# A new table of issue order and engine choice for block-causal attention with a feed-forward layer

## The chip, the cores and the metric

The kernel runs on one core of a Trainium2 chip. The metric is the device time of one execution in microseconds. The engines are named as in the profile: PE is the matmul engine (PEld its weight loads), DVE the vector engine, ACT the scalar engine, POOL the GpSimd engine; SP is a queue that only issues DMAs. ACT issues DMAs too.

## What is computed

Eight batches of eight heads, 576 positions, head size 64, float32. Attention is causal by blocks of 64, the result is laid out as 4608 tokens of 512 features, and a feed-forward layer of width 2048 follows, `(h * clip(h+3,0,6) / 6) @ w_out`.

```python
scores = scale * np.matmul(q, k.transpose(0, 1, 3, 2))
scores = np.where(block_i >= block_j, scores, -1e9)
attn = np.exp(scores - scores.max(-1, keepdims=True))
attn = attn / (attn.sum(-1, keepdims=True) + 1e-09)
x = np.matmul(attn, v).transpose(0, 2, 1, 3).reshape(B * S, H * D)
h = x @ w_in
out = (h * np.clip(h + 3.0, 0.0, 6.0) / 6.0) @ w_out
```

## The kernel before

float32 values are split into a high and a low float16 part, and a product is three float16 matmuls (high*high, high*low, low*high). Each is issued as two matmuls of 64 columns of the array side by side, which the profile shows as 128*64.

The work is cut two ways. Attention goes by slots: one slot is a pair of heads of one batch, 32 in all. The feed-forward layer goes by 13 pieces of up to 384 tokens, each with 16 column blocks f of 128. The first batch (slots 0 to 3) and the first piece are computed in float32 matmuls while the weights still arrive. A slot, with the tile names that the profile uses:

- loads `qk`, `vnat` (in the first batch `qf`, `qr`, `vnat`); `qk_prep` (line 727) splits q and k into `qks` and a transposing DMA on SP makes `qkT`;
- `s_group` (976): score matmuls `s`, maxima `st` on DVE, exponentials `p` on ACT, a POOL memset on `p`, the split into `phl` (high part on ACT or DVE, low part on DVE), a transposing DMA on SP to `pT` (`t_dma`, 1066);
- `pv_group` (1090): matmuls `pv`, and the split of the result into the piece's `x`.

The first batch has instead `sf`, `pf`, transposes `pt` on PE, copies `pT`, row factors `rd`, `rb`, and matmuls `pr` and `pf`. Weights arrive in 32 loads (`w_load`, 526: `rawi`, `rawo` or a borrowed `x` buffer). Each is taken through `exi`/`exo` on ACT and `sgi`/`sgo` on DVE or POOL into `win`/`wout`; later `w_split` (614) makes the high part on DVE, ACT or POOL and the low part on DVE. A block of a piece is `ffn1` (1304): matmuls `h`, `r` on ACT, `r` on DVE, `g` high on ACT or DVE, `g` low on DVE; then `ffn2` (1352): matmuls `o` into three PSUM buffers, and after the 16th block `osb` and the store. Pieces 11 and 12 use a product scheme with fewer matmuls (`h_pair`, 1244: tiles `m`, `hf`, `hu`; its operands `wr`, `wq`, `ws`, `xr`, `xt` from `w_comb` and `x_comb`). Forty matmuls on zeros (`warm`, 1599) are strewn into the beginning.

None of this order reaches the chip directly. A recorder notes 6437 steps in the order of the program, each with the engines that may do it (`scaled`, 275, `load`, 299, `plus`, 1193). The table `ORDER` (78 to 209) is a packed list of all 6437 step numbers with an engine for each, and `schedule` (340) issues them so:

```python
for lo, hi in zip(raw[:half], raw[half:]):
    o = self.ops[lo + 256 * (hi % 32)]
    o.eng = self.NAMES[hi // 32]
```

Each engine works its steps in the order of the table. DMAs stand in it too, on SP or ACT, and are issued in that order; a DMA that waits holds up all that stands behind it on its queue. PSUM is small: scores and `pv` rotate through 3 buffers, `h` through 2, `o` has 3 of its own.

Of the kernel before, what the change touches and what calls it, by code (L numbers as in the profile page):

```python
# [17 lines left out]
P = 128  # L18
# [6 lines left out]
U = 2.211  # L25
# [20 lines left out]
GA = 5  # L46
# [24 lines left out]
QP = 0.573  # L71
# [12 lines left out]
    "1q%xn{e3JWuPFQFtL?YQwHlh{aAX$QM>Ci#HfMufnT`7_traU39HPu^W7Zp3Q1;&mv?P(O{2cukdo0<#&Z?Dby&)^pC&(gT=|<~i"
    "Yn+@@j8hLT&#suwGqEZE!ZR^78~b2cc`?n98th_3qr0YiZkph`d57HdI&jE0BXp1HU9+|8s)~xMYf8fA&6yv5zipM~>WKB@rJ*0$"
    "Ik}Ucyz@UdUTe6zxi&8{yeT61-|-N2E#11pS%mW!+G9Jm)W^lYKAf<1?>^4OOPBixeP%}uY)ec^4!hFXwVivS=as^f{F9l!#yiek"
    "i0*3Y&dusQoOi_U>9gxMZr*x+yYOhti@w9z1v#-t6<Md>oPYB2*htT*W8M96Q%BAW|NZ{sC-aw-bl=&cZ@q7~D5uR6djI?BrQ^>A"
    "76|`)@bJ-)jEL-?caP`H)gG18N!1e-R>8}k)4xg-!>g%kJSX@sR#|clr(}3toOHuLf~-1!>DOh-)#kMeZ`#>YmrGJ^eZRlrnEudR"
    "CnE>iLp_lP&bJ-u_l`3Txwv*7+3HZ^?)J#z@f~8F<*xYjgjI>F*Ccsnj3x7{QoQ<eUk{vEnQrl>y0)g?Dq!3AV6kq;$-SrcZC|yc"
    "B=DW%uv5<b1v`UwmA-8`y?f6@*+}`{ipk0g4UHQ&?bq4-zO`+^!uA6P^O~Jy<eG&PPRhzFo;f@9L+$4;^%pOHYv3Nf%GLbyLFwZt"  # L90
    "mt;V;wy_ocWGpslN13H%&lCS_XkvQt(Vn(eiKCKKBPkj~n$9%y^$zp*%9zid$I5Fyu{b^<arT@`No&`w=WpOFSeQI_na}0A{55`y"
    "_G<6TTypS$i>ur6mGuQH_PZb2c>Y}B(tx6d{F34;Wu-xZ9>Ja=St+kl%R{p}w`_{6OiK@sh>DKc9a~Y=xN7U>rjV{}J6CVt(Y^CV"
    "&#pIDU%%bccCF=l@4FlAc$JY4s>2_L`W`=ddi&J8`NAT<r*6K#d#hD6u49(^v(ulRpLucrtgM{8!a~J+pI_3n=6ty``}?=AxCcL!"
# [1543 lines left out]
```

## Time and profile before

| | |
|---|---|
| Time, median of 3 runs | 986.66 us (985.13 to 988.3) |
| Span of the profiled execution | 983.9 us |
| PE busy | 967.0 us (98%) |
| DVE busy | 861.1 us (88%) |
| ACT busy | 667.7 us (68%) |
| POOL busy | 107.7 us (11%) |

The span runs from the first to the last instruction, so the profiled execution is 2.8 us under the median. Nearly all instructions have one line, L362, the helper that issues every step, so that groups are told apart by their tiles. PE counts as busy from a matmul's start to its modelled end; a busy PE can still be waiting, and the distance from one matmul to the next tells more.

### The profile page before, as it was taken

What the parts mean: (1) busy time and instruction counts of PE and PEld (TensorE: products, weight loads), DVE (VectorE), ACT (ScalarE), POOL (GpSimd) and SP (SyncE); (2) the same over time, 40 slices, a digit from 0 to 9 for tenths busy, and PEclk for the clock granted to TensorE, in tenths of its full rate; (3) what the DMA queues carried; (4) which work ended last, traced back from release to release, by engine and by line L of the source; (5) the groups of instructions that cost most, each with busy time, mean ns of one, the idle gap of its engine ahead of it and who ended that gap; (6) DMA issues with size and microseconds to landing.
All of it is one profiled execution on the core that took longest, in us unless ns stands there. A gap on an engine that the chain in (4) does not pass through costs nothing.

```text
span 983.9 us, 31140 instructions
## 1 busy us (share of the span) xinstructions
PE 967.0 (98%) x12625; PEld 702.0 (71%) x12625; DVE 861.1 (88%) x2330; ACT 667.7 (68%) x1610; POOL 107.7 (11%) x280
## 2 busy tenths in 40 slices
PE   8999999999999999999999999999999999999998
PEld 5676666677878876677677776777667766878774
DVE  5899999999998999999999888977888779986863
ACT  4788877877777677878776777677776564444423
POOL 1354210000100000100000010001100113000000
PEclk9999999999999999999999999999999999999999
DMA  8975479989779598898998697958566632000000
GB/s 234 296 224 152 85 149 158 176 154 201 135 124 218 99 184 161 162 165 155 160 162 151 124 176 124 154 113 157 98 143 118 108 71 47 2 33 3 35 2 34
DMA packets 407184, 129.04 MB, mean 131 GB/s; under 512 B 393984, under 2 KB 396544, under 8 KB 407040
## 3 DMA queue, kind: packets, MB, share of 16 engines
q1 hardware_dynamic: 399824, 121.75, 64.9%
q10 hardware_dynamic: 7216, 5.29, 1.9%
q8 instruction: 99, 1.62, 0.7%
q14 instruction: 45, 0.37, 0.1%
HBM read 45.09 MB, written 9.44 MB: 55 GB/s over the span
## 4 chain that ended last, share of the span: by engine, by line
PE 41%; DVE 7%; ACT 2%; DMA 1%; issue 1%; ACTq 0%; POOL 0%; DVEq 0%; POOLq 0%
PE o L362 18%; PE h L362 12%; PE m L362 5%; PE s L362 2%; PE pv L362 2%; DVE st L362 2%; DVE phl L362 1%; DVE g L362 1%; DVE r L362 1%; DMA pT<-phl 1%; ACT p L362 1%; DVE xt L362 0%; DVE x L362 0%; DVE ws L362 0%; ACT phl L362 0%
## 5 line engine op out<-in xcount | busy, mean ns | idle before, releaser
L362 PE MATMUL o<-wout,g 128*64 128x512 f16 (+3 forms) x3336 | 426.5, 378 | 1.7 <-ACT osb L362 1.4
L362 PE MATMUL h<-x,win 128*64 128x384 f16 (+2 forms) x3952 | 376.0, 319 | 0.8 <-DVE r L362 0.7
L362 PEld LDWEIGHTS <-win 128*64 128x64 f16 (+1 forms) x4440 | 259.9, 110 | 73.4 <-issue 1.6
L362 PEld LDWEIGHTS <-g 128*64 128x64 f16 x3360 | 204.7, 110 | 102.6 <-issue 1.7
L362 ACT ACTIVATE p<-s,st,esc 128x384 f32<-128x384 f32 (+5 forms) x280 | 163.0, 586 | 57.0 <-DVE st L362 45.0
L362 DVE SCALAR_TENSOR_TENSOR phl<-p,st,phl 128x256 f16<-128x256 f32 (+4 forms) x252 | 141.4, 581 | 7.2 <-ACT phl L362 6.5
L362 ACT ACTIVATE r<-h,eg,sh 128x384 f32<-128x384 f32 (+1 forms) x192 | 112.2, 598 | 43.7 <-PE h L362 40.2
L362 ACT ACTIVATE phl<-p,st 128x256 f16<-128x256 f32 (+4 forms) x190 | 103.3, 577 | 40.6 <-DVE st L362 21.0
L362 DVE TENSOR_REDUCE st<-s 128x1 f32<-128x384 f32 (+6 forms) x280 | 120.3, 447 | 7.5 <-PE s L362 7.0
L362 ACT ACTIVATE g<-r 128x384 f16<-128x384 f32 (+1 forms) x160 | 79.8, 504 | 56.3 <-DVE r L362 42.8
L362 DVE SCALAR_TENSOR_TENSOR g<-r,g 128x384 f16<-128x384 f32 (+1 forms) x192 | 103.2, 543 | 10.4 <-ACT g L362 9.8
L362 DVE SCALAR_TENSOR_TENSOR r<-r,eg,h 128x384 f32<-128x384 f32 (+1 forms) x160 | 93.6, 587 | 10.3 <-ACT r L362 9.5
L362 PE MATMUL s<-qkT 128*64 128x512 f16 (+7 forms) x1120 | 100.8, 287 | 0.6 <-DMA qkT<-qks 0.2
L362 PEld LDWEIGHTS <-vhl 128*64 128x64 f16 x1680 | 77.3, 110 | 19.4 <-issue 3.4
L362 PE MATMUL pv<-pT,vhl 128*64 128x192 f16 (+2 forms) x1680 | 85.2, 233 | 2.2 <-DVE x L362 1.1
L362 PEld LDWEIGHTS <-qkT 128*64 128x64 f16 x1120 | 59.0, 110 | 26.8 <-issue 3.1
L362 POOL MEMSET p<- 128x64 f32 x140 | 21.1, 160 | 480.0 <-DVE phl L362 368.5
L362 ACT ACTIVATION_READ_ACCUMULATOR p<-s,st,esc 128x1 f32 x280 | 55.2, 197 | 0.0
L362 ACT ACTIVATE r<-hf,eg,sh 128x192 f32<-128x192 f32 (+1 forms) x48 | 26.8, 593 | 40.1 <-DVE hf L362 32.9
L362 DVE SCALAR_TENSOR_TENSOR qks<-qk,rs_q,qks 128x576 f16<-128x576 f32 x56 | 46.0, 836 | 0.3
L362 PE MATMUL m<-x,ws 128*64 128x192 f16 x768 | 40.3, 246 | 0.1
L362 PEld LDWEIGHTS <-ws 128*64 128x64 f16 x768 | 35.3, 110 | 5.9 <-DVE hf L362 0.3
(196 smaller groups left out, 1056.6 us busy)
## 6 DMA issues: line engine op xcount, KB each, us to landing
out_dram<-osb SPq DMA_DIRECT2D x34, 256.0 KB, 2.8
qk<-in_q_dram SPq DMA_DIRECT2D x28, 288.0 KB, 4.2
vnat<-in_v_dram SPq DMA_DIRECT2D x60, 128.0 KB, 3.0
qk<-in_k_dram SPq DMA_DIRECT2D x26, 288.0 KB, 3.8
rawo<-in_moe_w_out_dram SPq DMA_DIRECT2D x11, 512.0 KB, 5.6
rawi<-in_moe_w_in_dram SPq DMA_DIRECT2D x6, 512.0 KB, 5.4
x<-in_moe_w_in_dram SPq DMA_DIRECT2D x6, 512.0 KB, 6.0
pT<-phl SPq DMA_TRANSPOSE x140, 3.9
```

The lines of the kernel that those rows point to most:

```text
L362: getattr(eng, method)(*args, **kw)
```

## The change

Only the table differs. The steps, their operands and buffers, and everything outside `ORDER` are the same.

```diff
 ORDER = (
-    "c-l=`1zc0_*QYxMj1m<XY;2767+}%eBW=1nRSdejRZK()lTuL-ySv3suv=2!^W4Gj{hw|3KF|5aInTY^yE{Kl%E-#g32DtypRJ)e"
...
```

Unpacked, both tables hold each of the 6437 steps once. Their order differs from the first entry on, and all five engines' sequences differ. 390 steps have another engine. The table below counts them by the matmul work that stands ahead of them in the old table (in us, a matmul counted as its columns at the dense distance in time that the rows below show).

| from, to | 0 to 50 | 50 to 200 | 200 to 700 | 700 to 922 |
|---|---|---|---|---|
| DVE to ACT | 8 | 28 (`phl` 14, `qks` 4, `g` 4, `x` 3, `pT` 2, `rb` 1) | 59 | 9 |
| DVE to POOL | 8 (`sgi` 4, `sgo` 4) | 8 (`qks` 4, `win` 2, `sgo`, `wout`) | 7 | 5 (`wr`) |
| ACT to DVE | 12 (`pT` 8) | 11 (`phl` 5, `g` 3) | 99 (`phl` 43, `g` 32, `x` 13) | 50 (`g` 25) |
| POOL to DVE | 2 | 2 | 1 | 2 |
| ACT to POOL | 7 (`rd`) | 17 (`wout` 6, `rd` 5, `win` 3, `qks` 3) | 9 | 0 |
| POOL to ACT | 10 | 5 | 0 | 0 |
| DMA, ACT to SP | 20 | 2 | 0 | 0 |
| DMA, SP to ACT | 9 | 0 | 0 | 0 |

The beginning of the two DMA queues (the digit is the slot, the letter the tensor where a tile holds both):

| | first entries |
|---|---|
| ACT before | vnat0, vnat0, qf0 q, qf0 k, vnat1, qf1 q, qf1 k, qr0 q, qr0 k, qr0 k, vnat2, rawi, then `p`, qf2 q, ... |
| ACT after | qf0 q, qr0 q, qf0 q, qf1 k, qf1 q, vnat1, qf1 q, qf2 k, qf2 k, then `p`, `p`, `p`, exi, ... |
| SP before | vnat0, qf0 q, qf0 k, vnat1, vnat1, qf1 q, qf1 k, qr0 q, vnat2, vnat2, qf2 q, qf2 k, rawi, ... |
| SP after | vnat0, qf0 k, qf0 k, vnat2, qr0 q, qf1 k, rawi, vnat3, vnat2, vnat2, qf2 q, qr0 k, qf2 q, qr0 k, vnat1, ... |

On PE 15 `warm` matmuls stand ahead of the first `qt` before, 31 after. At the end PE's last block group is `o` buffer 0 (512 columns wide, stored whole) before, and `o` buffer 2 (256 wide, its two halves done by ACT and DVE) after.

## Rows read from the trace of the kernel before

**Rows 1.** The page: busy time by engine; 40 slices of the span.
```profile
PE 967.0 (98%) x12625; PEld 702.0 (71%) x12625; DVE 861.1 (88%) x2330; ACT 667.7 (68%) x1610; POOL 107.7 (11%) x280
...
DVE  5899999999998999999999888977888779986863
...
PEclk9999999999999999999999999999999999999999
```
**Rows 2.** Busy time by stage: stretch, then PE, PEld, DVE, ACT, POOL, clock, DMA, GB/s.
```profile
0.00:70.00 70.00, 63.83 (x710) 44.72 (x711) 54.35 (x156) 47.09 (x131) 24.03 (x56) 1.00 0.84 254
70.00:233.00 163.00, 160.95 (x1872) 111.41 (x1872) 160.11 (x469) 131.92 (x328) 29.78 (x66) 1.00 0.79 152
233.00:980.00 747.00, 742.12 (x10049) 545.90 (x10045) 646.63 (x1708) 488.02 (x1151) 53.86 (x159) 1.00 0.64 115
```
**Rows 3.** Chain that ended last, three dense pieces: start, length, what, matmuls.
```profile
555.23 3.88 PE o L362 x36
...
571.20 0.97 PE h L362 x12
...
936.06 0.99 PE m L362 x24
```
**Rows 4.** Groups by shape: matmuls of the largest groups; busy, mean ns of one.
```profile
L362 PE MATMUL o<-wout,g 128*64 128x512 f16 x3156 | 396.6, 379 | 1.7 <-ACT osb L362 1.4 <-DVE g L362 0.3
L362 PE MATMUL h<-x,win 128*64 128x384 f16 x3456 | 330.2, 326 | 0.4 <-DVE r L362 0.2
```
**Rows 5.** Who DVE waited for, 70 to 233 us: total, times, longest.
```profile
DVE st L362 <- PE s L362: 0.9, 2, 0.8
DVE g L362 <- ACT g L362: 0.7, 1, 0.7
```
**Rows 6.** Tile views: ns of one, min/median/max, first and last start.
```profile
L362 DVE SCALAR_TENSOR_TENSOR wout<-exo,sgo x14: 670/680/1105, 22.5 to 88.6; 128x512 uint32<-128x512 uint32 x14
...
L362 POOL TENSOR_SCALAR sgo<-rawo x8: 658/696/1007, 31.6 to 96.2; 128x512 int32<-128x512 uint32 x8
L362 DVE TENSOR_SCALAR sgo<-rawo x5: 410/415/808, 38.8 to 82.5; 128x512 uint32<-128x512 uint32 x5
...
L362 POOL TENSOR_SCALAR qks<-qks x20: 670/976/1881, 102.8 to 775.9; 128x576 f16<-128x576 f16 x20
L362 DVE TENSOR_SCALAR qks<-qks x14: 281/301/341, 124.0 to 739.8; 128x576 f16<-128x576 f16 x14
...
L362 DVE TENSOR_SCALAR phl<-p,st x62: 265/414/565, 123.8 to 818.1; 128x512 f16<-128x512 f32 x19, 128x128 f16<-128x128 f32 x13, 128x256 f16<-128x256 f32 x12, 128x384 f16<-128x384 f32 x10
```
**Rows 7.** Groups by shape, 0 to 235 us, DVE: busy, mean ns, idle before.
```profile
L362 DVE SCALAR_TENSOR_TENSOR win<-win,rsio 128x512 f16<-128x512 f32 x14 | 11.1, 802 | 0.0
...
L362 DVE SCALAR_TENSOR_TENSOR wout<-exo,sgo 128x512 uint32<-128x512 uint32 x14 | 10.6, 760 | 0.0
```
**Rows 8.** Timeline of the beginning: start, length, engine, what, count.
```profile
1.06 3.38 PE L362 MATMUL warm<-zero 128*128 128x256 f16 x15 [1.06 <-DVE zero L362]
...
4.38 0.67 PE L362 MATMUL qt<-ident,qf 64*64 64x64 f32 x14
...
8.69 1.28 ACT L362 ACT_TABLE_LOAD   x1 [8.69 <-DMA qr<-in_k_dram]
...
9.99 0.31 ACT L362 ACTIVATE pf<-sf,st 128x64 f32<-128x64 f32 x1
```
**Rows 9.** Busy time in the head, in stretches of 5 us: columns as in rows 2.
```profile
10.00:15.00 5.00, 4.14 (x77) 2.84 (x75) 1.55 (x7) 3.16 (x12) 0.00 (x0) 1.00 0.88 259
...
25.00:30.00 5.00, 3.61 (x34) 1.79 (x33) 3.18 (x12) 3.88 (x17) 1.06 (x3) 1.00 1.04 352
```
**Rows 10.** Timeline of the end: start, length, engine, what, idle before it.
```profile
979.38 0.47 ACT L362 ACTIVATE osb<-o,so 128x256 f32<-128x256 f32 x1 [1.19 <-DVE osb L362]
...
980.30 0.69 ACT L362 ACTIVATE osb<-o,so 128x512 f32<-128x512 f32 x1 [0.45 <-PE o L362]
```
**Rows 11.** A DMA in the chain that ended last; who SP waited for.
```profile
486.08 7.10 DMA pT<-phl
...
SPq L362 <- DVE phl L362: 109.4, 31, 13.3
```

More of the change, by code (lines that the diff above doesn't have):

```diff
@@ L84 @@
[L84 to L93, printed above, removed]
@@ L204 @@
[L204 to L208 removed]
+    "c-n1vV_;+7*L9r~aZ(I}#%4RN-K0S=u5FEHYTIMmwr$(C?RTHd@A-dv&u#AAXYaMvUgsopb2FB|e*gJvVQFP;V{3=O+B-Np;qU|^"
@@ new lines @@
+    "iA<q7_&6rhoLyYqdiCz@5@Y4&+P_ynn-E4HYkJ>7L&bvyoZ(!FNG?<=EGWT2D*nu{e*NhTCd)l^2;LYFWpWyp${P@#mPyrlc@G@9"
+    "C^9xKAwE4L+PA8D^w_C^+7Y87Xj0jjh3aXg6N*aw{HITxlvq5&dA98wO^?2NZc@tRaZ_*}SkEn6?dQ+iVIZ`&*=04(>S)hi(?wdm"
+    "Zu?o{_`chYpXgJwci$=I+5@N0tk20i_pEL~?vjP%4b3OdUwE-}+4D=7SFf)w-(UNkwYby$Ap2VVld?q@F)a<(n<#G!?2bNq{M43;"
+    "-FbWWsXKS??b@?q<-7dP8}F}ru=?R;=Qr=Ku#dgmwAtN>X^;EhLi57=eEjkA6M^*C;+LhBgQM@@!pQe0fB$hUCoZX|v?h=7_8Da}"
+    "dTjimxWh-h{rqp-yv35r<X#G;n@ShaPd!oN5wl?Eu&-af1y2eI9U4pb^a~r1Ryc5(|MPII@1Xt+p;$0NG-Oy~QSrE5Z+j;sN>aGv"
@@ new lines @@
+    "(>Y1WS=rN~C*<&20|VBy@zeS=1?dgLM>gl0@{IZI9i2yyWn@N`EbZG>P?o;Dw4@~=vAQfZDS2{v)#T|@rdD(xpD}aR?6oPWx9{9t"
+    "w|+`b<-6lkr`6P5y0UBczWUmR6LU_^y|?$}<%%=+=goh$`6}ZPVZ-TD5Amg2w`|+-`i<=SkDtG)_H2K^EZ@KNt6Q&)2afDCRrl`0"
+    "`sQAV-M+)#VN=vO!G-f@FMj;6VrAs2)xRD8{B>eS%N5ED)#E2mpLxE>vi!{97Fm4yg5z!5$v<{**P)x&)B`ewqMCt&ckeuU;`GMd"
+    "9#&V+oV|YIR`xmZF3D{vWfS%A9!+uW+kSmFTRZ3Ur*EMBI8VB}hrA_b<(=y{FW9(R-V3x13JAVMbb0sQZqUUc!$({iHS$A9sCE^3"
+    "b>|w2Rk#jA4a;S^M;P=suC1>dJ*NJMk@jf(I2L<C-o*W5^V=TBKAkmbcEg;#9hb+ow=SCdY~Q>C!@Pq+IvSh4j~`M{*gU_Yt7YxF"
@@ new lines @@
+    "1#MSm^mI?3d1%n##Y@YVFWUR@)90UG{vQ0bwY~D|AL7e6hh<AvJo)_%uX=86!LYG?V0`h)%hB#SMosd+|1hAJ&m<?8U>?CQ)YpR>"
+    "=*q$Joo{H|=z?S7<qM@tg`WGjNsi0xalQM*iwpw>_C0a(^&7>YWcd{3v{Qpel}?S>KD@H3s=91d#*ouzYDV{)SUb4?<lKfaV@*Tr"
+    "qgJ0iceHb1)3UDE?sfS&c?An1#bM!VwS!CI;u8{+bVnN3tnZ1KK4XJ^<II%Q%;piBW^c}#)iTF(OZ3IL`wHO`Hh#jZk&+#Q(&im_"
+    "IREv6gOATYfBB+y$?|iLsOdLvEpmBs`{|uShqIsEee-tY07pxwrBWQ8vf}-R3-<_`WtZGM2KHK<IArL@VPAf`%HraQTCw&02kC4t"
+    "Nu5;o?vr<4Khna_0bc_X63H3GSNp8|)>}^N=j$(5{P>x~NDc{A&ze1FuJX{~BQd(m^ecbD{zmj?vQ$9^<GlId?p8;+JX40V4gc72"
@@ new lines @@
+    "TRVYpeo89blfK`%dsd(3UdZM|RyZgpEQp%2aN@M+dnK8Rv$9LajGCIBQ#MKQtGvQu^!=jB#fz?u&CFd=*V)zGGdV9mYxsz&>g<|Y"
+    "zR!c5f``HDH*T6PoN)fajF}TBO@4my(umlm=2J^HT)DitpuV-O{R#F(&grMuwoO@@d*kZ$Wun(p?OV2N-Cq6vgvjFMNzXIS-Z;M9"
+    "x8qgA{tq7y?ArZq&m*T5D)q`$t3RzFQP!^e{N*>*l3aCbuhlnen)BG@D@NMH#@WW-bb0*!4-TL5<LB*P1h**7fP_Scfgb%_d)W~&"
+    "Gkf>xd+=*h^J-ROSZZ0pl{DSTaAu2^-Qmv(D2m`FB?krtuUX5=ujyY%HLlYe{+5q4ZQCAs_1g9IwRNo<O52KukD68!QcJI^Z*Ta}"
+    "_^~7US!l_p(VzDp*t2(Eb<DWV8((+_^A6qIdU!;izW0vy`_;9hd&|xv8#m3Fdu;Qa{`8@{hRt$kczOHy-k!~zK4X;M*WEqG@BX|n"
@@ new lines @@
+    "{<p;m#*bTn&I(1uF{E!ky-)T!HCXBU*RtN~v{*tu=XX0a%q`^Nb9Mulf5}GmQvLmvwXNN}*Kf|hz5l?S<A8y0k?x0K@80tsJ;pwX"
+    ")+D^3Jf+!RPfU{f%K`=rmpcchU%so0P`G$_>J4*;Wu!O;xz0;I<FzU{E!8;C6qA`XdRk-@D{e@_p!o|rOBR-vmG7>o6b#*yy>wCY"
+    "*zJ2)B(7`?Uw$-)a4Pp)UVhWzrv>9ruhJHdxqI(^Y)et`vhxqlc(Xr0Kl^ZB&yfokr_Y$#*50vt|D?%D$zN_fI*`JdwOA_q*-O4="
+    "eeVggr#zmccyjE@rX}mvZrBK4DF<(jd$wbzQk8mg+?}nL4t?mG_O)L|`sJJ3u>C)M`yKvE`~A;f-HnKw`kAwCSy&pfGOu1sa35gv"
+    "!kQbuc?;p?tEsO)T1~X2#8Yq68yN$C*bRAuA-;V#J3Dvqds@z%xy~-|(d&vCK4|E8=7^CVk@mapxK40#U`3A_?HT3fH;l)h7dORA"
@@ new lines @@
+    "AQTz%NZvRf)0na9q<CL(AlZN7q}t+flk4go8(K8UDdXLiEnl&+H9xpLBsR35a6+o2v1!NFfRduA({QVHZr_!bzAbJyp0K*A`XsTu"
+    "f<&&|yKn!-O`C(}FK{g_+ta#m-P;ds@3tH``2N^pd`D+SSNGZGp6SOA9d4O)Zi%1&k&ovuT(q+O^nKC#Kbe<iEVZ%y{H0ewn3uQR"
+    "*KZW6=$cp}g^y-P;D+m$uVVgAzHM>ml+TpckAC^C`SJ62=;>);;a6(z>hCQy7^leOx`_J^)|Nb;SN7!TeA9wgk?4_PQJ-gh9TzWI"
+    "{>I7SIc=%N!*kiJ7p2$%FK64&nY)7Ea<q!RlEXZ4=G5tdXU;mGV_06fT5YsgwSL3-8g10WL4*7CA3}zIJG|PuYu8mbZVs)eFYi~W"
+    "zIZu!^%~PAI`>w~)Ug-df8z2K{Er_#D+NNPF*;`Wh<?NRw|NRh4ejENPW9$*v0Wp(M-?}(Wdw~bIxyzomaOca>0iHmKg5z8<|mtS"
@@ new lines @@
+    "a`S#P&G?fa`Sb6u-`lpg9XTqn+%d{Zx^q|K?K?6#d-u%I1%<~H@R1ujY@L_)apeOa)s{i~whp(kjf&nsQWLZFq#fqOo{fWVjTtf4"
+    "{q~bPcjNa)#(CVk|Ly_jaTL}*;o;jyIF~nX*TVDGfY`)=Lz2=-zR^819iBcrZasrO-Er3Q7i3Dt?3b^$rKG0KnLE$v^y>L1Ucbr9"
+    "FDMKOK3TN%Oh{ICap-pE9WkeJasvaXJ9qD*9X>Mr=z@idrcNtg{P0ohSwl%_xc2drJ$_}!_GRwf??3U}`IW0qRaULhos3w0q2>D1"
+    "XJ0!%>2Fj_c>dzb)q|hEEg>DSY+keW%lCEttBEzWb@dIGE{`)m0`}>P9t?l1-#otkC*>FQ_p;@iUTrvCK_hPLx_0PY(EAT(f<r<_"
+    "VH=yyjtL9@_$NJM#a|2ii#OGoS)Ljk&EuTXs$)WOio?Var0z+R8O#BL2EU{#tZf9gc9$>%hm5Qgil#)QrVaJ;AI%Z_^u)h*RvB0c"
@@ new lines @@
+    "?!I+oZS2&<B#LC3GdCc6n3t|$Y+Q+pYdu?<Q|h>&k;g~7F}<m|Mc=k>f9rvRhh*~hqN?2L!{-++swwjhym4{y?IlY)y31G9c6Qx-"
+    "R6OqTI=A&3#&0~asrRipuX{G%xpd{)mX&kg+>3g<>?&v8a_;nZefsvhZee+M#j*P{f6bcxV8;8c+qQq$@o=a8@gqlf?f&xo_n*gp"
+    "Pp$Usjeat~Jsh5|`~zO}r@#Ex>-&$t*3U%!;w2wH{cN?7CfGWCO-xFb$;EaGHIAp6lff4V`^;a+{(NB!CMJ+I<JEj?jnad$)XPDe"
+    "lDcR#Gi#-1wqtHB79X^D$g=k319M7B%kqW}8#HcJVOT+MW_f;5ovtlH9}+s*U^GQmtoHUvFP^x$W6k*bhRP``wp9%uF=_3Xu_M=w"
+    "8XY@t>Vm;F>l>R|o7?v6t?t~gF>ONJzL}eT{`&TP|EwSFI}h$U`rG%!$y0w0Y`JmouSNIyj?-t(zPB8E?nzfHJVac$c<IpLB~Q2S"
@@ new lines @@
+    "ICitI!>7**)wAcx>ZHrlW?#Ab!1jyPiz8oOzDg}T?!=jEopMcS<92`R>+6|Wx9l}(Hyqw@dD)K!^FQ?R@EkC35Rp_=EU?2|8|LPn"
+    "n<vcodMLu--wuHv7ax1eb7;=x6_x%~y~erp?&Df8{$1ahH35M^A=SHQ-Ma4Bum4c`gw<>NuUlWj5GOKO>HDwOZirYjDr4f5sRXIE"
+    "S#qOk@U-CHp|VNt?9$0C8#iz9xye|LUGaG3Af~(C(As7+Ic>dl`_3l%D#ycNQ7m{`F4K*C^Y+NQ_eZxK>pFfS{Dbd^2EWMd2cmm+"
+    "?EEYepE|v3w`9QGlQ9Q5?BU$T>9hCn=6wA0<!fEHOs<HkkCx7zw_yIlGc(SfyLoHxA--VW&zZlJxBuK(GUMJ|%X{~QDl0X9(dF|O"
+    "tQQkf1`Z~Y65ytmnDoGte4j#n^Z<TcrKLZ-f?0O;;iD(X5knq7#SO}M{N!)y)6A@F?4+UJzURJNx8arJto8QK;C}GK;(1P9{<G&V"
@@ new lines @@
+    "NG}RrJCP~lH@=)O(P3Ii>87%auxZ1*&|@5J_MFMyK0Bst-MnSn_V3hJuiwBeZsgqgZ}pd^?%eh6y`Kbb8oNiie);fm{(`;xXi{f|"
+    "Z2v+R-$fyN4vd0_gkZHv?jL$Z`Qv9m;8%?b-mrPgR}B0%W^~Xn;~>M}1!3V=kB%8K)GPAW@5m^0`}{L9zNM-<V3Dt%zqd~y+#Xi1"
+    "S-Ub%n?JT*$A~D<7ZwG@HpO*zHLqii-?4bf`lZXp6;B!)TQXtdbVFQx>4vh635g5W9zT8X(BY|zXRLy6uT4hNk<D8oqod9={CaWp"
+    "Sklh3=azP_*|z=V)924#y?zTnKHu$fd)WBs)Ya7|uLV24N4KEIPk!&-vt(J%n?FB$T{%Ad(}%5lS7FYd`1tGF=ij~glP~m(A&wl)"
+    "a<`v$Ou(K}&f$uL;xAui-+Pnj4cPuaE?(mCrINpm=^5EMWDCp8tlSakr>|V0@qio2<>ZvVsd;u5Y0Bo7);5*8sMvGBxKZut)PeIX"
@@ new lines @@
+    ">!O(lLOLTekavzM*1(qh8)~FXGuzfU!#+5B0tVI&t3u282Qrt@Hqtcch;;E(gSp6P7Y|4}LjsyX5T!9=BZ~pv^>0_;1@9}(8HAnH"
+    "YG)0sL4z!45XKDAzy_j=*%-<>yLd!tTtM5!!z1cn);Y>K>K_9oG#VF=fB52m0xr&QM7u!M1uD@{?sn05ctnFnbhJj};Syc!((Mur"
+    "g3;X?q^t3Oi$}Bzz@s$?1``htnEnGnWd1{0m*{9H!4zc8Rdn|F7no7d0!_?FbT$J~-mDPqF%HG%8JYqZ+D1ov{D(kPkAHw@vr4qf"
+    "e=WxS*UQCh$ip?-)x*^VPB2_i(beo3CNYTb;_B(?664|F=?Z}>oZ#ZwgJv-(`tO2HF+Hv^kcdGjGb{$>{+q=hx*3nAP;&iG%zOX|"
+    "Q9b|DbT#8*{-@;n@6YpJL)6kNX)ee7FXQ^J#eY&}%D+BlQ=b3qn>+oZp(XrZdsi^;+Jjp5{6CutJU0"
```

199 lines of the change are left out of this document (80 added, 119 removed).

## The prediction

> **What bounds the kernel now.** I read the page first, then busy time by stage, then the chain that ended last, then who waited for whom, and last the two tables, unpacked.
>
> The page says PE 98% busy, and a reader might stop there, with nothing to win from an order [rows 1]. But a matmul counts as busy until its modelled end. The chain gives the dense distance: 36 `o` matmuls in 3.88 us, 12 `h` in 0.97, 24 `m` in 0.99, so 108, 81 and 41 ns each [rows 3]. That is their columns at 2.4 GHz, two side by side; the granted clock is full throughout [rows 1]. The two largest groups alone are then 3156 * 0.108 = 341 us and 3456 * 0.081 = 279 us [rows 4]. All matmuls of the program, counted so by their columns, come to 922 us. I call this matmul work. It is the same in both tables, so an order can win at most 984 - 922 = 62 us, and some 1.2% of the work, 11 us, is pitch above the columns that even the dense pieces have (3.88 us where 36 * 512 / 2 / 2.4 GHz is 3.84). About 50 us remain.
>
> Where they are I find by laying the matmul work against the times at which the trace starts the same steps. The first 50 us of work end at 70 us, the first 200 at 233, all of it at 980. So the head loses 20 us, the next stretch 163 - 150 = 13, and the long rest 747 - 722 = 25, of which 9 are the pitch. In the stretch from 70 to 233 the DVE is busy 160.1 of 163 us [rows 2] and waits for next to nothing [rows 5]. There the DVE is the bound: it splits weights, scores and values all at once. After 233 it has 647 us of work for 747 [rows 2], and PE sets the pace. In the head neither engine is full; the DMAs move 259 to 352 GB/s at 88 to 104% of their time [rows 9], and ACT's first instruction starts at 9.99 us, since 12 DMA issues stand ahead of it on its queue [rows 8].
>
> **The change, part by part.** I count what each table puts on the DVE, with the durations of this trace, each less its overlap with the instruction before.
>
> *From 50 to 200 us of work.* 36 steps leave the DVE, 12.4 us, the largest share 14 high parts `phl` at a median of 0.41 us [rows 6], and 13 come to it, 4.1 us. Net the DVE has 8.3 us less, so 160.1 - 8.3 = 151.8 us. The matmul work here is 150 us, with the pitch 151.8. The two are level, and neither can be covered fully by the other, so I put the stretch at 156 instead of 163: **7 us less**. The bounds are 11 less (nothing but the pitch left) and 0 (PE finds another wait). A second count supports it. For each matmul I take all DVE work that stands ahead of it on the DVE's own queue and is needed, directly or through that queue. At 125 us of work it is 134.2 us before and 124.1 after; at 200, 203.7 and 199.0. Before it exceeds the matmul work by up to 9 us, after it doesn't.
>
> *The head.* ACT has 9 DMA issues ahead of its first instruction instead of 12, some 2 us at about 0.6 us each. The data that must be issued before the matmul at 30 us of work are 7.5 MB after and 12.9 before; before, that matmul starts at 48.5 us, which is 266 GB/s, just the rate of the head. Against it stand 31 `warm` matmuls ahead of the first real one instead of 15; 15 take 3.38 us [rows 8], so the first real matmul could move from 4.4 to 6 or 8 us. I take **3 us less**, between 8 less (some 40% of the 20 lost) and 3 more (the `warm` matmuls in full).
>
> *POOL.* It gets 61 steps from ACT and DVE and gives up 22, in all 38 us more by its own durations; 15 of them come before 200 us of work. It has 54 us of work in 233 [rows 2], so it has room. But it is slow: `qks` takes 0.98 us there against 0.30 on the DVE [rows 6]. And it disturbs: `wout<-exo,sgo` on the DVE takes 680 ns in the median and up to 1105 [rows 6], so that the mean is 760 [rows 7]. The excess of mean over median of such groups, 14 * 0.08 + 14 * 0.06 and the like, is near 3 us beside 48 us of POOL work; 15 us more make **1 us more**. Bounds 0 and 9 (the 21 steps that POOL gets net before 200 us, each at 1105 - 680 ns).
>
> The Trainium skill has a rule on this (SBUF — State Buffer, Who interferes with whom): DVE and GpSimd share a pair of ports under an exclusive lock, a DVE instruction in a fast two-port mode or with two SBUF inputs takes it, and the later one blocks fully. The trace agrees in kind, with 1105 ns where 680 is usual and 1881 for a `qks` on POOL where 670 is the least. By that rule every POOL step could cost the DVE a wait, and the upper end above would hold; by the means it is the lower.
>
> *From 200 us of work to the end.* 166 steps move, and the DVE gets 9.0 us more up to 700 and 8.4 after that: 664 us in 747, still below PE. These cost nothing while PE sets the pace; without that cover they would cost up to 17. What decides here is whether PE finds its operands. For every matmul I compared the PE work that stands between it and the last matmul behind its operands with the durations of the chain between. Past the first 100 us, 101 matmuls have less before and 117 after; the deepest shortfall is 1.7 us before and 3.7 after (blocks near 236 and 530 us), and the deepest of each 100 us add up to 12 and 17 us. On the other side the DVE is no longer behind on entering this part. I take **2 us more**, between 8 less and 10 more.
>
> *The end.* The last store waits for an ACT instruction of 0.69 us before and of 0.47 after [rows 10]: **0.4 us less** with the wait ahead of it.
>
> *Sum.* -7 - 3 + 1 + 2 - 0.4 = -7.4 us. The span would be 983.9 - 7.4 = 976.5; with the 2.8 us by which the median stands above the span, the time is 979.3, in round numbers **979 us**.
>
> **The rivals.**
>
> *The DVE's gain goes to POOL's collisions.* If each of the 21 net steps before 200 us costs the DVE 0.42 us, 9 us come back where 1 is in the sum: 979.3 + 8 = 987 us, no change. It speaks for it that the DVE is 98% busy just there, against it that the observed excess is a tenth of that. 0.17, together with a gain that is lost to any other wait in the same place.
>
> *PE starves in the long rest.* This is the rival on the other side. The transposes of `phl` go through SP in order, one took 7.1 us in the chain, and SP waited 109 us for `phl` in all [rows 11]. In the new order a quarter of the `s` and `pv` groups have less PE work behind them than before. If each of the 117 short matmuls, which stand in some 25 clusters, stopped PE by the mean of the deepest (about 2 us by cluster) less the half that PE loses there now, 25 us come on top of a rest that was counted with 2; that is 979.3 + 23 = 1002 us. It decides as soon as the rest gives up more than the 11 to 12 us won ahead of it. Against it: PE lost only 16 us there with 101 short places. 0.13.
>
> *The head doesn't move, or gets worse.* With 3 more instead of 3 less it is 985 us, again no change; it is counted with the first rival.
>
> *More comes free.* If the head loses 12 instead of 20 us and the stretch after it only the pitch, 5 + 4 more, and the rest 5 less, it is 965 us. 0.12.
>
> That the change doesn't do what it says can't be: the table decides both the order and the engine of each step.
>
> **How the numbers follow.** Forecast (972 to 983.7) 0.58, more 0.12, no change 0.17, slower 0.13. Likeliest is 979. The range for 8 in 10 runs from 968, which leaves out most of the case of more, to 990, which takes in no change and leaves out the starving. A measurement of this kernel can tell about 0.3%, 3 us, from no change. Faster by more than that: 0.58 + 0.12 = 0.70; within it 0.17; slower 0.13.
>
> **What would show it.** The DVE's busy share from 70 to 220 us should fall from 98% to about 96 or less, with waits for PE in it. The 200 us of work should end near 223 instead of 233, and the step at 50 near 67. The rest should take 745 to 750 us as before. POOL should be busy about 145 us and DVE 869. The prediction is wrong if the head takes longer than 72 us, if DVE instructions of the weights show means well above 0.8 us, or if PE has waits of 2 us and more for `pT`, `g` or `x` after 233.

## The result and the profile after

| | before | after |
|---|---|---|
| Time, median | 986.03 us (985.13 to 988.3, 4 runs) | 995.59 us (993.77 to 996.77, 4 runs) |
| Span of the profiled execution | 983.9 us | 995.0 us (its time 996.77) |

The ratio is 1.0097 (95% interval 1.0079 to 1.0116): 9.6 us slower, where 979 us, 7.4 less, was forecast. The forecast was wrong in sign, and the time lies above its range. The traces are further apart than the medians, 11.1 us instead of 9.6. An execution's time is some 1.8 us above its span, so the traced execution of before ran a little under its median and that of after is its slowest. (The 2.8 us that the prediction added to its span hold both things, the 1.8 and an execution under the median.)

The page of after: busy time by engine, the DVE's slices, and the clock, which answer to [rows 1].

```profile
PE 972.1 (98%) x12625; PEld 694.0 (70%) x12625; DVE 893.5 (90%) x2377; ACT 633.8 (64%) x1524; POOL 140.6 (14%) x319
...
DVE  4899999999999999999998989889988989897864
...
PEclk9899999999999999999999999999999999999999
```

The DVE is busy 32 us longer and ACT 34 us less. The forecast was 869 us for the DVE and 145 for POOL. One slice, from 25 to 50 us, has a lower clock; before has none.

Busy time by stage of after, columns as in [rows 2], which it answers to.

```profile
0.00:70.00 70.00, 64.29 (x709) 45.75 (x710) 51.05 (x153) 45.11 (x123) 25.10 (x56) 0.95 0.71 217
70.00:233.00 163.00, 161.38 (x1846) 108.07 (x1848) 158.68 (x442) 136.41 (x335) 45.63 (x85) 1.00 0.83 167
233.00:980.00 747.00, 735.11 (x9965) 534.24 (x9962) 678.75 (x1773) 447.99 (x1061) 69.82 (x178) 1.00 0.62 115
```

In the middle stretch the DVE is still busy 158.7 of 163 us, although the prediction counted 8 us of steps off it. In the last it has 32 us more than before.

Where the time went shows when the matmul work of the prediction is laid against both traces again. The table gives the start of the step that stands at so much work, and PE's waits of over 60 ns (the gap between the end of the work issued and the next matmul), summed by stage.

| matmul work | start before | start after | difference | PE's waits up to here since the row above, before / after |
|---|---|---|---|---|
| 50 us | 69.5 | 70.3 | +0.8 | 18.7 / 20.3 |
| 200 us | 232.8 | 234.3 | +1.5 | 9.8 / 10.6 |
| 700 us | 749.7 | 757.3 | +7.6 | 7.1 / 13.3 |
| 900 us | 957.3 | 968.6 | +11.3 | 3.9 / 7.6 (to the end) |

So in these traces the head and the next stretch, from which 10 us were to come, gave nothing. The rest, which was to lose 2, lost 9.8. Whom PE waited for there, first before, then after, from 233 us on: total, times, longest.

```profile
PE o L362 <- ACT osb L362: 1.4, 1, 1.4
PE pv L362 <- DVE x L362: 1.1, 1, 1.1
```

```profile
PE pv L368 <- DVE x L368: 4.6, 5, 1.4
PE s L368 <- ACT p L368: 3.6, 4, 1.6
PE m L368 <- DVE hf L368: 0.6, 1, 0.6
```

Both large groups are waits for a PSUM tile that `x` or `p` still reads. Matmuls that waited for a transposed `pT` have 0.2 us before and 0.3 after, and the transposing DMAs land as fast as before (`pT` in 3.8 us against 3.9, `qkT` in 6.8 against 7.7).

### The profile page after: what moved, and what is told of

It reads as the page before. It is cut to its first block, busy times and chain, and to the rows that moved or that the text cites. A ratio compares the mean times of both kernels' runs of the same rounds, so it can differ in the third digit from the quotient of the medians.

```text
span 995.0 us, 31198 instructions
## 1 busy us (share of the span) xinstructions
PE 972.1 (98%) x12625; PEld 694.0 (70%) x12625; DVE 893.5 (90%) x2377; ACT 633.8 (64%) x1524; POOL 140.6 (14%) x319
## 5 line engine op out<-in xcount | busy, mean ns | idle before, releaser
L368 PE MATMUL o<-wout,g 128*64 128x512 f16 (+3 forms) x3336 | 419.4, 378 | 0.4 <-ACT osb L368 0.3
L368 PE MATMUL h<-x,win 128*64 128x384 f16 (+2 forms) x3952 | 368.4, 319 | 1.7 <-DVE r L368 1.2
L368 PEld LDWEIGHTS <-win 128*64 128x64 f16 (+1 forms) x4440 | 257.1, 110 | 80.7 <-issue 4.0
L368 ACT ACTIVATE p<-s,st,esc 128x384 f32<-128x384 f32 (+6 forms) x280 | 163.1, 586 | 73.3 <-DVE st L368 59.4
L368 DVE SCALAR_TENSOR_TENSOR phl<-p,st,phl 128x256 f16<-128x256 f32 (+4 forms) x252 | 146.8, 589 | 4.8 <-ACT phl L368 3.2
L368 PE MATMUL s<-qkT 128*64 128x64 f16 (+7 forms) x1120 | 100.0, 287 | 4.4 <-ACT p L368 3.6
L368 PEld LDWEIGHTS <-vhl 128*64 128x64 f16 x1680 | 73.1, 110 | 19.9 <-issue 6.5
L368 PE MATMUL pv<-pT,vhl 128*64 128x192 f16 (+2 forms) x1680 | 78.9, 233 | 5.3 <-DVE x L368 4.6
L368 ACT ACTIVATE g<-r 128x384 f16<-128x384 f32 (+1 forms) x122 | 60.8, 502 | 31.9 <-DVE r L368 18.7
L368 POOL TENSOR_SCALAR qks<-qks 128x576 f16<-128x576 f16 x40 | 32.6, 823 | 99.7 <-ACT qks L368 34.4
```

The source lines that it names most:

```text
L368: getattr(eng, method)(*args, **kw)
```

## The experiments

Each time is the median of a kernel's executions. The ratio behind it, with its 95% interval, compares them with executions of the kernel before on the same chip; it is taken over all executions and differs from the quotient of the two medians by up to 0.0015. After itself stands at 1.0097; in microseconds 0.1% is 1 us. A difference between two ratios, each with an interval of about 0.002 on either side, is known to some 2 us.

### Engines without their order

Three kernels change the engine of steps in one stage and leave the order as it is. `work` is the matmul work ahead of a step; DMAs keep their queue.

```diff
-table = [(o, before[o]) for o in order_before]
+table = [(o, after[o] if 50 <= work[o] < 200 else before[o]) for o in order_before]
```

> The order of before, and of its steps between 50 and 200 us of matmul work the 71 that change their engine on the engine of after (36 off the DVE, 13 onto it, net 8.3 us less on the DVE); nothing else changes. Theory of the prediction (the DVE, 98% busy there, is the bound): the stretch from 70 to 233 us shortens by 5 to 7 us, time about 980. Rival (PE waits there for single chains that are late, whose steps do not lie behind a queue on the DVE; a full DVE only works ahead): the time stays within 2 us of 986, and the DVE is as busy as before because it takes later steps sooner. Second rival (POOL's steps slow the DVE's): the DVE steps that are the same in both take 3 to 5 us more in sum, and the stretch stays or gets longer.

Measured: 1000.64 us, ratio 1.0123 (1.0106 to 1.0141), 12 us slower. Its trace is 16.6 us longer than that of before; 7 of them are lost between 50 and 62 us of work and 7 more up to 200. PE's waits from 60 to 250 us:

```profile
PE pr L362 <- POOL rd L362: 3.2, 1, 3.2
PE h L362 <- DVE r L362: 1.3, 2, 1.1
```

`rd` went to POOL at a place in the order that was chosen for ACT, and stands there behind POOL's weight steps. None of the theories had this. That wait, and the clock at 0.5 from 84.1 to 90.9 us right behind it, make nearly all of the first 7 us; the other 7 are not traced to a step.

```diff
-table = [(o, before[o]) for o in order_before]
+table = [(o, after[o] if 200 <= work[o] else before[o]) for o in order_before]
```

> The order of before, and of its steps behind 200 us of matmul work the 241 that change their engine on the engine of after, so that the DVE gets the 27 us more of busy time that after shows there. Theory of the load (the late PSUM releases of after come from the work that the DVE got from ACT): 5 to 9 us slower than before, 991 to 995, with waits of PE for x and p. Theory of the order (they come from matmuls that after places too close behind the chain that they need): within 2 us of before.

Measured: 1029.4 us, 1.0415 (1.0394 to 1.0436).

```diff
-table = [(o, after[o]) for o in order_after]
+table = [(o, before[o] if 200 <= work[o] else after[o]) for o in order_after]
```

> The order of after, with the engines of before for all steps behind 200 us of matmul work (243 steps). Theory of the load: most of the 9 us that the rest lost come back, 987 to 989. Theory of the order: 993 to 996, with PE's waits for x and p at the same places as in after (about 405, 585, 669, 793 and 819 us). If each does half, 990 to 992.

Measured: 1042.62 us, 1.0540 (1.0515 to 1.0564).

Both theories fall at once: either mixture in the rest is four to six times worse than after. An engine choice is good only at the place that the order gives the step, so these runs don't divide the loss between order and load. They show that the two halves of a table can't be judged apart, which is what I did when I priced the moves by their durations.

### The seam

```diff
-table = after
+table = [s for s in after if work_after[s] < 200] + [s for s in before if work_after[s] >= 200]
```

> Order and engines of after for its steps ahead of 200 us of matmul work, then order and engines of before for all others. If the loss of after lies wholly behind 200 us, as the two traces say: 986 to 988.5, with the step at 200 us of work 1 to 2 us later than before and the rest as long as before. Rival (the head of after leaves the DVE or the transfers a debt that the rest pays): 991 to 995.

Measured: 993.91 us, 1.0056 (1.0034 to 1.0079). In its trace the step at 194 us of work comes 1.2 us later than in before, the one at 206 us 7.1 later, and the one at 900 us 8.4: six of the eight are lost within 12 us of work, at the seam, where steps pile up that the old table has earlier and the new one later (PE waits 2.5 us for one `g` there, and behind it the clock is at 0.5 from 240.2 to 243.7 us). Behind it the old rest takes 1.3 us more than in before. That fits a loss that belongs to the new order of the rest, but the seam itself is an artefact, and the rival isn't excluded by this run alone.

### What the DVE's work costs between 50 and 200 us

The prediction rested on the DVE as the bound here. Three kernels keep order and engines of before and change the load alone.

```diff
 for method, args, kw in o.ways[o.eng]:
+    if o.n in THIN:
+        method, args, kw = "memset", (args[0], 0.0), {}
     getattr(eng, method)(*args, **kw)
```

> The kernel before, order and engines untouched, but 16 of the DVE steps that make low parts of the weights (win and wout, between 52 and 108 us of matmul work, 0.74 us each, 11.8 us in all) are replaced by a memset of zero in the same place on the same queue, so the low parts of these weight blocks are left out of the computation. That takes about 8 us off the DVE and nothing else changes. Theory of the prediction (the DVE is the bound from 70 to 233 us): 6 to 8 us faster. Rival (PE waits for single late chains there, a full DVE is not what holds it): 0 to 2 us faster, and the DVE shows idle time in the stretch.

Measured: 985.27 us, 0.9988 (0.9970 to 1.0006): between 3 us faster and 0.6 slower. The executions differ with the granted clock. The eight in which its mean was 0.999 or more took 984.6 us in the mean, where the thirteen such executions of before took 986.9; the three at 0.993 to 0.998 took 987.9 to 991.5. So where the clock stays up the removal gives 2 to 3 us, and nowhere the 6 to 8. The traced execution is one of the three (987.91 us). Its row of the stretch, and the two rows of 5 us in which the gain is lost:

```profile
70.00:233.00 163.00, 159.42 (x1837) 112.19 (x1837) 153.05 (x464) 131.70 (x328) 28.43 (x64) 0.99 0.80 150
```

```profile
155.00:160.00 5.00, 2.82 (x42) 1.91 (x39) 3.95 (x11) 3.62 (x11) 0.00 (x0) 0.95 1.26 178
160.00:165.00 5.00, 5.00 (x54) 3.06 (x52) 2.29 (x11) 2.79 (x6) 0.00 (x0) 0.71 0.50 107
```

The DVE has 7 us less work and 10 us idle, as intended. What ended the idle time of the matmuls that read `qkT`, from 100 to 165 us:

```profile
  DMA qkT<-qks: 2.4, 1
  DVE r L366: 2.2, 1
```

PE is 2.2 us ahead of before at 122 us of work, and then at 156.7 us it stands still for 2.2 us for the scores `s` of slot 6. Their weight loads wait for `qkT` (the first line), and the matmuls start with them (the second, which the profile puts down to the DVE's last step). This `qkT` was issued only 1.6 us earlier than in before and landed 9 us after its issue. Behind the wait the clock is at 0.71 in the mean of 5 us, and in this execution the gain is gone. The place where the next wait ends was not in my sum.

```diff
 for method, args, kw in o.ways[o.eng]:
     getattr(eng, method)(*args, **kw)
+if o.n in TWICE:
+    for method, args, kw in o.ways[o.eng]:
+        getattr(eng, method)(*args, **kw)
```

> The kernel before with 15 DVE steps between 50 and 200 us of matmul work (low parts of phl and g, 7.7 us in all) issued twice, at the same place. If the DVE is the bound there: 6 to 8 us slower. If it has room that the busy share does not show: under 3 us slower.

Measured: 993.04 us, 1.0075 (1.0055 to 1.0094): 7.4 us for 7.7 us of work, by the interval 5.4 to 9.3. Added work costs most of its time or all of it, taken work gives back about a third where the clock stays up and nothing where it falls. So in this stretch the DVE is level with at least one other chain, and a busy share of 98% shows only that it would hurt to add.

The same edit with 20 POOL steps in `TWICE`:

> The kernel before with 20 POOL steps between 50 and 200 us of matmul work (sgo, sgi, qks, rd, 15.2 us in all, about what after adds there) issued twice, at the same place; no step leaves or joins the DVE. Theory of the collisions (a DVE step that falls on a POOL step waits for it): the DVE steps of the stretch get some 4 us longer in sum, as in after (excess over the usual length 3.0 us before, 6.9 after), and the time rises by 2 to 4 us. Rival (a collision is absorbed like any other delay): under 1.5 us slower.

Measured: 995.4 us, 1.0078 (1.0060 to 1.0095). The DVE's steps of the stretch took twice as much above their usual length as in before (about 6 us against 3, worked out as in the table further down), nearly as in after. But in the trace 4.8 of the time lost lies between 50 and 62 us of work, where `pr` waits 2.2 us for the doubled `rd`, which is a POOL step on PE's own chain, and the clock is at 0.5 behind that wait from 85.5 to 88.9 us; some 2 us come elsewhere. That more POOL work makes the DVE's steps longer is confirmed; what it costs in time isn't separated from the price of a longer chain.

### What more work costs the DVE in the rest

The same edit with 30 DVE steps in `TWICE`, behind 200 us of work.

> The kernel before with 30 DVE steps behind 200 us of matmul work (low parts of phl and g, 17.8 us in all, 9.6 up to 700 us and 8.2 after) issued twice: as much as after adds to the DVE there without collisions. Theory of the load: 6 us slower or more. Theory of the order (the DVE has room there, 87% busy): under 4 us slower, most of it in the first half, where the DVE is above 95%.

Measured: 999.69 us, 1.0115 (1.0094 to 1.0136): 11.4 us for 17.8, about two thirds. In the trace 6.6 us of it are lost up to 700 us of work and 4.9 behind, so no more where the DVE is fullest than elsewhere. It falls out against "these cost nothing while PE sets the pace", and against my theory of the order. A DVE that is 87% busy on average has no room where a chain needs it next.

### Single places of the new order

Here the new table is kept, and steps are moved by a few places. First the head. PE's waits from 10 to 40 us of after, then the DVE's from 18 to 27:

```profile
PE pt L368 <- DVE pT L368: 2.1, 2, 1.7
PE pt L368 <- ACT pf L368: 1.2, 1, 1.2
```

```profile
DVE vmax L368 <- DMA vnat<-in_v_dram: 1.8, 1, 1.8
```

And busy time of after in stretches of 2.5 us, the clock third from the right:

```profile
22.50:25.00 2.50, 0.95 (x18) 0.61 (x14) 0.96 (x3) 1.28 (x5) 1.05 (x3) 1.00 0.92 322
25.00:27.50 2.50, 2.35 (x20) 1.38 (x24) 2.50 (x10) 1.98 (x8) 1.35 (x6) 0.74 0.98 314
27.50:30.00 2.50, 2.09 (x12) 0.67 (x5) 1.73 (x5) 0.00 (x0) 0.65 (x1) 0.50 0.84 266
30.00:32.50 2.50, 2.50 (x13) 2.21 (x12) 1.49 (x8) 1.57 (x6) 0.41 (x2) 0.50 0.93 328
```

The new table has a `vmax` step on the DVE ahead of the load that it reads. The copies `pT` stand behind it, PE stands behind them, and soon after that the clock is granted at 0.5 for five us, which is 1.2 GHz.

```diff
 rb0_0 <- pr0_0
-vmax0 <- vnat3
 pT2_0 <- pt2_2
 st3_1, st3_0, st3_2
 pT2_0 <- pt2_2
 pT0_1 <- pt0_3
+vmax0 <- vnat3
```

> The kernel after with one DVE step moved: vmax of vnat3, which in after waits 1.8 us for its load at 24 us while the copies pT that PE needs stand behind it on the DVE, is issued six DVE steps later, behind those copies. Theory (this wait stops PE for 1.6 us, and PE's clock is granted at half from about 27 to 33 us after it): about 3 us faster than after, 991.5 to 993, no fall of the clock between 25 and 35 us, and 50 us of work done 2.5 to 3.5 us earlier than in after. Rival (PE is held there by the transfers in any case): within 1 us of after.

Measured: 993.94 us, 1.0062 (1.0045 to 1.0078), 3.5 us better than after's ratio (1 to 6 by the intervals). The same stretches:

```profile
22.50:25.00 2.50, 2.14 (x28) 1.38 (x26) 2.24 (x8) 1.85 (x10) 1.50 (x6) 1.00 0.94 312
25.00:27.50 2.50, 1.63 (x12) 0.57 (x13) 2.50 (x9) 1.18 (x5) 1.10 (x4) 1.00 1.04 325
27.50:30.00 2.50, 2.37 (x19) 2.07 (x20) 2.17 (x10) 1.96 (x7) 0.92 (x3) 1.00 0.99 290
```

The clock stays full, and 50 us of work are done 3.3 us earlier than in after, 2.5 earlier than in before. But one trace of each doesn't settle what the step costs, since the head varies from execution to execution. The other runs begin with the same heads:

| head | clock stays full | clock falls to 0.5 |
|---|---|---|
| old | 69.1 to 69.6 (4 traces) | 69.8 to 72.5 (4) |
| new, `vmax` in its place | 67.2, 68.0 | 69.5, 70.3, 71.2 |
| new, `vmax` moved | 67.1, 68.2 | 68.6 |

The table gives the start, in us, of the step at 50 us of work. In the five of the middle row `vmax` waits 0.4 to 2.3 us for its load, and the clock falls behind the three longest waits. Where it stays full, the new head is some 1.8 us faster than the old one, whether `vmax` was moved or not; and four of the eight old heads fall too. So the step itself costs little, the clock behind it as much as the new head wins or more, and the 0.8 by which the traced head of after is behind is in part the chance of which executions were traced.

Next the five waits of `pv` for `x`. The last of them in the trace of after, start and length first:

```profile
818.12 0.35 DVE L368 TENSOR_SCALAR x<-pv 128x192 f16<-128x192 f32 x1
818.50 0.36 DVE L368 SCALAR_TENSOR_TENSOR x<-pv,x 128x192 f16<-128x192 f32 x1
...
818.92 0.44 PE L368 MATMUL pv<-pT,vhl 128*64 128x192 f16 x6 [1.16 <-DVE x L368]
```

A `pv` tile is filled in two parts, and `x` of the first columns doesn't touch the second. Yet the matmuls of the second part start 0.06 us after the end of that `x` (818.86). In all five places `x` stands ahead of the second part in the table.

```diff
 pv31_0 first part
-x <- pv31_0 first columns, high and low
 pv31_0 second part
+x <- pv31_0 first columns, high and low
```

> The kernel after, but at the five places where PE waits inside a pv group for x, the x steps that read the first columns of the group's PSUM tile stand behind the matmuls that write its other columns instead of ahead of them. In the trace of after PE waited 1.60, 0.60, 1.08, 0.77 and 1.36 us at these places. Theory (the wait comes from the order alone, since a matmul into a tile waits for every earlier reader of it): 4 to 5.4 us faster than after, about 990 to 991.5. Rival (the DVE is too full there, the waits come back behind): within 1.5 us of after.

Measured: 994.12 us, 1.0070 (1.0058 to 1.0083), 2.7 us better than after's ratio (0.5 to 5 by the intervals); 0.5 us of such waits are left from 233 us on, of 4.6 in the profile's count:

```profile
PE s L368 <- ACT p L368: 3.2, 3, 1.6
PE h L368 <- DVE r L368: 1.5, 4, 0.6
...
PE pv L368 <- DVE x L368: 0.5, 1, 0.5
```

The order alone made these waits, as the theory says; of the 5.4 us (the waits at the five places, from the end of the work issued to the next matmul) about half came back elsewhere, as the rival says.

Then the collisions at the end. A DVE step of one element per row, and the POOL step beside it, in after:

```profile
840.75 2.08 DVE L368 SCALAR_TENSOR_TENSOR so<-pw_v,egm 128x1 f32<-128x1 f32 x1
```

```profile
840.50 2.31 POOL L368 TENSOR_TENSOR wr<-win 128x1024 f32<-128x1024 f16 x1 [7.31 <-DVE wq L368]
```

The same step takes 0.15 us elsewhere. Here it starts inside the POOL step and ends with it (842.83 and 842.81).

```diff
-wr2, wr3, wr4, wr6, wr7: POOL
+wr2, wr3, wr4, wr6, wr7: DVE
```

> The kernel after with the five wr steps that it moved from the DVE to POOL (1.2 us each on the DVE, 2.1 to 2.6 on POOL) back on the DVE, at their places in the order. The DVE gets 6.1 us of work and loses the 7 us that its steps beside these five took longer. If the collisions cost what the trace shows: 0.5 to 2 us faster than after. If the work of the steps themselves counts as much: within 0.5 us of after. If the DVE's queue is what counts: 1 to 4 us slower.

Measured: 995.21 us, 1.0081 (1.0061 to 1.0100), not to be told from after. From 700 to 900 us of work it loses 3.5 us on before where after loses 3.6. The DVE's excess in that stage fell from 15.7 to 8.6 us, and the steps themselves came back with 6.1: the two cancel.

Now the places together: the two moves above, `wr` on the DVE, and three more at which PE waited. One is on ACT: `r8_5` needs a buffer that `osb` uses too. The chain of after, start, length and what:

```profile
661.63 4.35 DMA out_dram<-osb
665.98 0.02 issue
666.01 0.03 ACT r L368
...
667.87 0.66 ACT p L368 x2
668.53 0.04 issue
668.57 1.06 PE s L368 x10
```

ACT waits for the store, the exponentials behind it wait with ACT, and PE waits 1.7 us for their PSUM tile.

```diff
-r8_5 (ACT, both halves)
 p26_4, p26_5 (ACT)
+r8_5 (ACT, both halves)
...
+x <- pv28_1
 phl30 (DVE)
-x <- pv28_1
...
+hf11_2
 ws6 (DVE)
-hf11_2
```

> The kernel after with the vmax step moved as in the other run, the five x pairs moved as in new_pv_late, and four more local moves at places where PE waited behind 200 us of work: the two ACT steps of r8_5, which wait for a buffer that is still being stored, behind the exponentials that s26_2_1 needs (1.7 us); the x of pv28_1 ahead of phl30 on the DVE (0.75 us); hf11_2 ahead of ws6 on the DVE (0.8 us); and the five wr steps back from POOL to the DVE (collisions of 2.0 us with so12 and others). Theory (the loss of after sits in a dozen places of the order, not in the engines' loads): 985 to 988, level with before. Rival (the DVE's larger load in the rest is the cause, and each mended place moves the wait on): 990 or more.

Measured: 988.22 us, 1.0007 (0.9997 to 1.0017). Some twenty steps moved, of 6437, the five `wr` among them, give back 8.9 of the 9.6 us (7 to 11 by the intervals). Not all of it comes from the rest: in the trace it still loses 3.2 us on before from 200 to 900 us of work, where after loses 9.8, and the head stands 1.0 ahead.

```diff
+hu11_2
 ws6 (DVE)
-hu11_2
...
+r1_3
 eg8 (DVE)
-r1_3
...
+st31_1_2
 phl30_8 (DVE)
-st31_1_2
```

> The kernel new_mended with three more waits taken away: hu11_2 ahead of ws6 on the DVE (1.4 us of PE's waiting in new_mended), r1_3 ahead of eg8 (1.0), the maximum of s31_1_2 and its scaling ahead of phl30 (1.8). If single places are all that the new table loses: 984 to 986.5, under the kernel before by 2 to 4 us. If each mended place now uncovers the next wait, as in old_mended: 987 to 989, level with before.

Measured: 987.39 us, 1.0005 (0.9987 to 1.0022): three waits of 4.2 us taken away, and no further gain. The same was tried on the old table:

```diff
-x <- pv31_0 first columns
 pv31_0 second part
+x <- pv31_0 first columns
...
+osb4_2
 p16_8 (ACT)
-osb4_2
...
-vmax4
 r3_12 (DVE)
+vmax4
```

> The kernel before with six local moves at places where its own trace shows PE waiting: x of pv31_0 behind the matmuls into the same tile (1.27 us), osb4_2 ahead of an exponential on ACT (1.59), vmax4 behind r3_12 on the DVE (0.65), x of pv11_1 ahead of phl12 on the DVE (0.67), two rd1_2 ahead of sgo6 on POOL (0.36), r10_5 ahead of g10_7 on the DVE (0.28). If waits of this kind are what the order can win, 3 to 5 us faster than before, 982 to 984; if each only uncovers the next wait, within 1.5 us of before.

Measured: 987.82 us, 0.9993 (0.9978 to 1.0009). Its rival holds by the time, but one of the six moves didn't do what it was meant to. The step `osb4_2` before, and in this kernel:

```profile
420.71 0.69 ACT L362 ACTIVATE osb<-o,so 128x512 f32<-128x512 f32 x1 [1.55 <-DMA out_dram<-osb]
```

```profile
423.23 0.69 ACT L362 ACTIVATE osb<-o,so 128x512 f32<-128x512 f32 x1 [2.60 <-DMA out_dram<-osb]
```

It waits for a store that still reads its buffer. Ahead of the exponentials it only waits longer, and PE, which waited 1.6 us behind it, still waits 1.4. So some 3.4 of the 4.8 us were taken away, and against them stands a wait of 2.0 us for `qkT`.

## Why the prediction was wrong, point by point

The forecast was -7.4 us; the traces show +11.1. The largest misses are 7.7 us behind the head and 7.8 in the rest, then 3.8 in the head.

**The stretch behind the head: -7, measured +0.7** (164.0 us from 50 to 200 us of work against 163.3). The step that failed is "there the DVE is the bound". The busy share of [rows 2] was read as a limit whose relief comes back as time. Taking 7 us off the DVE without touching anything else gave 1.2 us in the ratio, 2 to 3 where the clock stayed full, and left the DVE idle for 10; adding 7.7 cost 7.4. The lower bound that the prediction named, 0 because PE finds another wait, was the true value. The run with work taken off shows one such wait, the chain of `qkT`; which chain holds PE there in after itself no run shows. The second count, of DVE work that must precede a matmul, had the same fault, since it counts one engine. The share from 70 to 220 us, which was to fall to 96% or less, is 97% (145.8 of 150 us).

**The head: -3, measured +0.8.** With full clock in both the new head is some 1.8 us faster, below the 3 foreseen. What the step left out is the clock: it fell in the traced execution of after, behind a DVE step that stands ahead of its load, and not in that of before. Of its own terms one failed: nine DMA issues instead of twelve were to let ACT begin 2 us earlier. In after:

```profile
6.81 0.92 PE L368 MATMUL qt<-ident,qf 64*64 64x64 f32 x24
```

```profile
4.88 0.48 ACTq L368 DMA_DIRECT2D qf<-in_q_dram  x1
7.77 1.12 ACTq L368 DMA_DIRECT2D qf<-in_k_dram  x2
8.92 1.28 ACT L368 ACT_TABLE_LOAD   x1 [8.92 <-DMA qf<-in_q_dram]
10.22 0.31 ACT L368 ACTIVATE pf<-sf,st 128x64 f32<-128x64 f32 x1
```

The last two issues, of `qf2`, come right behind the first `qt` matmuls, which read the buffer that `qf2` takes (there are two), and these start at 6.81 us instead of 4.38 behind the 31 `warm`. So ACT begins at 10.22, not earlier than the 9.99 of before. The other term came out better than feared: leaving the `warm` matmuls out, 5 us of work are reached at 16.8 us instead of 17.8.

**POOL: +1, measured more, and in a stage that was left out.** I worked out for both traces how much longer each DVE step took than the median of the same operation and shape, where that is over 20% and 50 ns; all such steps lie beside a POOL step.

| DVE excess, us | to 50 | to 200 | to 700 | to 900 | sum |
|---|---|---|---|---|---|
| before | 2.7 | 3.0 | 1.7 | 6.1 | 13.5 |
| after | 1.2 | 6.9 | 6.6 | 15.7 | 30.4 |

The weight steps by which the prediction wanted to tell a collision, [rows 7], got shorter instead (means of 760 and 802 ns before):

```profile
L368 DVE SCALAR_TENSOR_TENSOR win<-win,rsio 128x512 f16<-128x512 f32 x14 | 10.5, 753 | 0.4 <-ACT win L368 0.4
...
L368 DVE SCALAR_TENSOR_TENSOR wout<-exo,sgo 128x512 uint32<-128x512 uint32 x14 | 9.7, 702 | 0.5 <-ACT exo L368 0.4
```

Up to 200 us of work that is 2.4 more, within the bounds of 0 and 9. Behind it there are 14.5 more, which no term of the sum held: `wr` and `qks` on POOL were counted for the early part only. These 17 us are half of the 32 by which the DVE is busier; the steps that come to it net, at their median lengths, make 11 of the other half. What the longer steps cost in time isn't shown: with `wr` back on the DVE 7 of the 17 us were gone, and the time stayed. The Trainium skill (SBUF — State Buffer, Who interferes with whom) states that the later one blocks fully, and that a `tensor_reduce` on the DVE never contends; the trace agrees with both: `so` ends with `wr`, and of 48 reductions that lay beside a POOL step (memsets left out) for more than 0.1 us none was long, where 30 of 108 `scalar_tensor_tensor` were.

**The rest: +2, measured +9.8**, at the upper bound of 10. Two steps failed. "These cost nothing while PE sets the pace": 17.8 us more cost 11.4 in the old order. And the count of short chains took the dependences from the columns that steps read and write; a matmul into a PSUM tile waits for every earlier reader of the tile, so that the order itself adds waits which no count of data showed (4.6 us of `pv` behind `x`). At its deepest shortfalls, near 236 and 530 us, PE waited for no operand that came late; the waits near 530, of 0.6 and 1.1 us, are for `x` in the tile. (The 166 steps that the prediction lets move here are those between 200 and 700 us of work that join or leave the DVE; 241 move in all.) Of the three signs that it gave for being wrong only the last showed, and only in sum: 4.6 us of waits for `x`, the longest 1.4.

**The end: -0.4, measured -0.2.**

**The rivals.** PE starving in the long rest, 0.13, came nearest: it had the sign and the place, but 23 us where 9.8 were lost, and the wrong mechanism, transposes on SP ([rows 11]), where PSUM tiles were released late. The collisions that eat the gain were there, but there was little gain to eat.

What stays open is how the rest's loss divides between the DVE's load and the order. Some twenty moves brought two thirds of it back in the trace, and with the head nearly all of the time, while the DVE's load stayed, so the load alone doesn't explain it; but each mended place also gave less than its wait.

## What to carry to other kernels

A busy share near 100% says that more work will cost (here it did at 87% too); whether less will help is told only by the chain that is late next. A run that takes work away tests it, if enough executions are looked at to tell the chain from the clock. In a new issue order look first for the step that stands ahead of its own load or behind a store, with others queued behind it, and for matmuls into a tile that an earlier step still reads: some twenty of them made up nearly all of the 9 us here. Engine and place of a step are one choice, and a price per step moved, taken at its old place, has no sign.

## What the runs showed of the hardware that was not expected

The clock can fall behind a single wait of PE. In the trace of after PE waits 1.7 us, works 0.95 of the 2.5 us around that wait, and then has the clock granted at 0.5 for five of the next eight us, in an execution whose other slices show full clock. It isn't certain to fall: of five traces with this head three show it and two don't, and of eight with the old head four do. Executions of one kernel differ by this: those of after at a mean clock of 0.997 took 995.2 to 996.8 us, the one at 0.999 took 993.8. A DVE instruction of 128x1 can take 2.08 us instead of 0.15 beside one POOL instruction.
